# Mixer kernel on one core: two weight groups take one token set first, and the other set is turned by VectorE from stored rows

## The chip, the cores and the metric

The kernel runs on one core of a Trainium2 chip. The time is the device time of one execution in microseconds (us); a run's time is given as the median of several executions. TensorE is called PE, VectorE DVE, ScalarE ACT, GpSimd POOL and SyncE SP, as in the profile.

## The reference

For 2048 tokens u of width 576 (all float32):

```python
xn = layernorm(u)
s  = causal_conv(xn, kernel made from log_A, A_imag, C, log_dt) + xn * D_skip
y  = layernorm(xn)
h  = gelu(y @ w1 + b1)          # 576 -> 4608
g  = silu(h @ w2 + b2)          # 4608 -> 576
out = u + s * g
```

The convolution is a state-space kernel of length 2048 per channel, computed here with Fourier transforms on PE.

## The kernel before, in words

**The two-layer network.** Each float32 product is made of three fast matmuls: an operand is split into a high part (a copy rounded on ACT) and a low part (the rest, on DVE), and high x high, high x low and low x high are summed. The 2048 tokens are done in two halves of 1024, and a half in two token sets of 512. The hidden width 4608 is cut into 12 groups of 3 x 128 units. One group on one set is a slot; there are 48. The order of slots is group by group, set 0 then set 1 (line 1436). A slot has a first layer (`layer1`, L508, 42 matmuls of 512 columns into three hidden blocks) and a second layer (`layer2`, L565, 72 matmuls of 288 columns, each third one with the low part of a hidden block), whose four results DVE adds to `acc` (L573). Between them ACT makes the activation (L541) and the high part `hh` (L544), DVE the low part `hl` (L547), block by block. The weights of a group come by SP in eight parts to a ring (`load_raw`, L448 to L453) and are split by ACT (L488) and DVE (L485) while PE works on the other layer; a new part is loaded when an old one in its place has been split (line 486). 24 groups of weights are loaded, 12 for each half.

**The tokens of a set** must stand with their features on the partitions, as `XH`, `XL` and `XR` (the last 64 features). `norms` makes normalised rows (`second`, L386). In the first half PE turns the rows (`y_transpose`, L413: 4 transposes for each of 5 feature blocks), ACT takes the high part from PSUM (L417, L419) and DVE the low part (L423, L425); `turn_lines(4, 1)` places this for set 1 within slot 0. In the second half the rows are stored to DRAM (`y_s`, L388), loaded in pieces by token blocks (L1231, 32 x 16 x 32 elements) and turned by DVE in blocks of 32 x 32 (L1236).

**The convolution** has a chain of its own: parameters (`params`: four arrays loaded by SP in L681, turned by DVE in L688), tables, kernel spectrum, and on PE short matmuls with small tiles of the array (L869, L941, L979, L1032, L1059), which stand as 87 stretches between the matmuls of the network, the first in slot 9, the last in slot 44. Fifteen of the 87 hold two steps, the others one.

**The order of the work** is made when the program is built. `Order` keeps lines of steps, each with an engine, an allotted time, needs and a due time, and a clock for each engine. PE's matmuls of the network are placed one after another; steps of the other engines go where they begin earliest without making a step with a due time late; `pe_turns` puts convolution and turning steps between the matmuls, at a pace that spreads them up to END = 1020. Loads are steps without an engine: SP's queue gets them in the order in which the planner comes to them, and works them off in that order. Each engine runs its instructions in order.

## Time and profile before

| what | us |
|---|---|
| median of 3 runs (1082.5 to 1084.62) | 1082.88 |
| profiled execution | 1082.74 |
| its span in the profile | 1081.0 |
| PE busy | 1071.7 (99%) |
| DVE busy | 947.9 (88%) |
| ACT busy | 650.7 (60%) |

Busy times are sums over instructions that may overlap on an engine. The span runs from the first to the last instruction; 1.7 us of the execution lie outside it.

### The profile page before, as it was taken

How to read it: one execution, taken by the hardware profiler on the slowest of the kernel's cores; microseconds unless marked ns; L12 is line 12 of the kernel's file. 1: busy time of each engine (PE TensorE's matmuls, PEld its weight loads, DVE VectorE, ACT ScalarE, POOL GpSimd, SP SyncE). 2: the span in 40 equal slices, each digit the busy share in tenths (PEclk: the TensorE clock that was granted, in tenths of full speed). 3: DMA queues.
4: the chain of work that ended last, by engine and by line, in shares of the span. 5: the costliest groups of instructions: out<-in, count | busy, mean ns of one | idle time of the engine just before them, and what ended most of it. 6: DMA issues, size and time to landing. Idle time of an engine off the chain costs nothing.

```text
span 1081.0 us, 27198 instructions
## 1 busy us (share of the span) xinstructions
PE 1071.7 (99%) x11491; PEld 933.9 (86%) x11491; DVE 947.9 (88%) x1518; ACT 650.7 (60%) x974; POOL 199.1 (18%) x281
## 2 busy tenths in 40 slices
PE   9999999999999999999999999999999999999997
PEld 7989999889888888888888888888888887888896
DVE  7797878989999999999999999999999996677366
ACT  6558569767666665767756666576665754233333
POOL 6559342110000200002100010000100022110231
PEclk9999999999999999999999999999999999999999
DMA  7746455823225221455523433142312347332344
GB/s 236 229 140 190 163 186 196 229 71 113 72 71 110 65 80 55 112 94 129 144 59 100 82 86 88 33 124 55 97 53 76 115 85 237 111 111 88 89 156 117
DMA packets 136537, 125.54 MB, mean 116 GB/s; under 512 B 88156, under 2 KB 108096, under 8 KB 135392
## 3 DMA queue, kind: packets, MB, share of 16 engines
q1 hardware_dynamic: 120624, 76.44, 26.2%
q0 software_dynamic: 15040, 46.40, 13.8%
q8 instruction: 90, 1.47, 0.6%
q10 hardware_dynamic: 752, 0.97, 0.3%
q14 instruction: 31, 0.25, 0.1%
HBM read 95.52 MB, written 34.01 MB: 120 GB/s over the span
## 4 chain that ended last, share of the span: by engine, by line
PE 98%; DVE 1%; issue 1%; DMA 0%; ACT 0%; POOL 0%; ACTq 0%; POOLq 0%; DVEq 0%
PE mxa L508 22%; PE mxa L565 21%; PE mxb L565 21%; PE mxb L508 21%; PE cv L869 3%; PE cv L979 3%; PE cv L1032 2%; PE cv L941 2%; PE cv L1059 1%; DMA idp<-in_ident_dram 0%; PE mxa L523 0%; PE cv L413 0%; DVE A L646 0%; DVE row L386 0%; DVE acc L573 0%
## 5 line engine op out<-in xcount | busy, mean ns | idle before, releaser
L565 PE MATMUL mxa<-w2h,hh 128*128 128x288 f32 x573 | 171.3, 299 | 0.0
L565 PE MATMUL mxb<-w2h,hh 128*128 128x288 f32 x576 | 170.9, 297 | 0.0
L565 PE MATMUL mxb<-w2h,hl 128*128 128x288 f32 x576 | 170.0, 295 | 0.0
L565 PE MATMUL mxb<-w2l,hh 128*128 128x288 f32 x576 | 169.6, 294 | 0.0
L565 PE MATMUL mxa<-w2h,hl 128*128 128x288 f32 x573 | 169.1, 295 | 0.0
L565 PE MATMUL mxa<-w2l,hh 128*128 128x288 f32 x573 | 168.7, 294 | 0.0
L547 DVE TENSOR_TENSOR hl<-h,hh 128x512 fp32r<-128x512 f32 x144 | 99.4, 692 | 76.8 <-ACT hh L544 76.1
L541 ACT ACTIVATE h<-mxa,b1t 128x512 f32<-128x512 f32 x73 | 50.2, 690 | 126.3 <-PE mxa L508 121.7
L769 POOL DMA_DIRECT2D par<-par_s x36 | 27.3, 759 | 519.4 <-DVE mg L812 479.7
L565 PEld LDWEIGHTS mxa<-w2h,hh 128*128 128x128 f32 x573 | 107.6, 188 | 9.4 <-issue 6.3
L565 PEld LDWEIGHTS mxb<-w2h,hh 128*128 128x128 f32 x576 | 108.2, 188 | 4.9 <-issue 2.5
L565 PEld LDWEIGHTS mxb<-w2l,hh 128*128 128x128 f32 x576 | 108.1, 188 | 0.6
L565 PEld LDWEIGHTS mxa<-w2l,hh 128*128 128x128 f32 x573 | 107.6, 188 | 0.7
L565 PEld LDWEIGHTS mxb<-w2h,hl 128*128 128x128 f32 x576 | 108.1, 188 | 0.0
L565 PEld LDWEIGHTS mxa<-w2h,hl 128*128 128x128 f32 x573 | 107.5, 188 | 0.0
L541 ACT ACTIVATE h<-mxb,b1t 128x512 f32<-128x512 f32 x71 | 48.9, 689 | 76.9 <-PE mxb L508 76.1
L544 ACT ACTIVATE hh<-h 128x512 fp32r<-128x512 f32 x144 | 90.8, 632 | 4.0
L573 DVE TENSOR_TENSOR acc<-mxa,acc 128x576 f32<-128x576 f32 x88 | 65.4, 743 | 17.0 <-PE mxa L565 16.7
L508 PE MATMUL mxa<-XH,w1h 128*128 128x512 f32 x284 | 80.2, 404 | 0.0
L508 PE MATMUL mxb<-XH,w1h 128*128 128x512 f32 x280 | 77.1, 397 | 0.0
L508 PE MATMUL mxa<-XL,w1h 128*128 128x512 f32 x284 | 76.2, 390 | 0.0
L508 PE MATMUL mxa<-XH,w1l 128*128 128x512 f32 x284 | 76.0, 389 | 0.0
(231 smaller groups left out, 2420.8 us busy)
## 6 DMA issues: line engine op xcount, KB each, us to landing
raw<-in_B_w_dram SPq DMA_DIRECT2D x72, 288.0 KB, 3.3
raw<-in_B_w_dram SPq DMA_DIRECT2D x96, 192.0 KB, 2.9
par_s<-A POOLq DMA_DIRECT2D x8, 1080.0 KB, 5.9
par<-par_s POOLq DMA_DIRECT2D x36, 240.0 KB, 3.3
f2t<-f2q SPq DMA_DIRECT2D x24, 256.0 KB, 3.7
raw<-in_B_w_dram SPq DMA_DIRECT2D x48, 96.0 KB, 3.6
u_s<-in_A_u_dram POOLq DMA_DIRECT2D x16, 288.0 KB, 4.3
xc<-xn_s SPq DMA_DIRECT2D x48, 96.0 KB, 3.8
```

The source lines that it names most:

```text
L508: nc.tensor.matmul(q, a, b, start=j == 0, stop=j == len(ops) - 1)
L541: nc.scalar.activation(t, q, AF.Gelu_apprx_tanh, bias=b1t[:, g * G + i:g * G + i + 1], scale=1.0)
L544: LAST[0] = nc.scalar.activation(hh[:, i], t, AF.Copy)
L547: nc.vector.tensor_sub(hl[:, i], t, hh[:, i].bitcast(F32))
L565: nc.tensor.matmul(q[:, dh, :288], a[:, i, c], b[:, i, d], start=i == 0 and k == 0, stop=i == G - 1 and k == 2)
L573: nc.vector.tensor_add(o, q[:, dh:dh + n, :288], b if g == 0 else o)
L769: nc.gpsimd.dma_start(PAR[b].rearrange("p (g i) k -> p g (i k)", g=4), dram(par_s, (b // 6 * CH + b % 6 * 4) * NPAR, [[D * NPAR, P], [24 * ...
L869: nc.tensor.matmul(q[32 * g:32 * g + 32, i // 2, i % 2 * 64:i % 2 * 64 + 64], U[:, ri, 4 * g + i, :], v[:, ri, 4 * g + i, :], start=ri == ...
L941: nc.tensor.matmul(Q1ST[i, x][g // 2][64 * f:64 * f + 64, g % 2].rearrange(order), f1t[r].rearrange("p s k -> p (s k)"), rhs(r, f), start= ...
L979: nc.tensor.matmul(Q[i][32 * q:32 * q + 32, f, 2 * ri:2 * ri + 2], m[r, 4 * i + q, 32 * ri:32 * ri + 32], A2[r, 4 * p + 2 * i + q // 2, :, ...
L1032: nc.tensor.matmul(QI[q // 2][64 * f:64 * f + 64, q % 2, i], MAT["g2t", p + i // 2][r, i % 2, ri], YS[p + i // 2][0][r, i % 2, ri, f], sta ...
L1059: nc.tensor.matmul(Q[f][32 * e:32 * e + 32, t], g1t[r], A2[r, k:k + 2, 1].rearrange("p i d r -> p i r d"), start=True, stop=True, skip_gro ...
```

## The change

The order of slots becomes a table: groups 0 and 1 on set 0, groups 2 to 11 on both sets, then groups 1 and 0 on set 1; the second half begins with group 0, whose weights stay, and goes on with groups 1 to 11. So set 1 is first used in slot 3 instead of slot 1, and there are 25 loads of a group's weights instead of 24.

Set 1 of the first half is no longer turned by PE. `second` writes its rows with the first 512 features in another order (two instructions for a row: 4 x 4 x 32 elements and 64), SP stores them to a new `y4_s`, and `row_lines` loads them again: for each block of 128 tokens four loads of 32 x 4 x 128 elements (pieces of 512 bytes, L1225 in the new file), and for the last 64 features two loads of 32 x 16 x 32 (L1228). DVE turns them (L1234, L1237), ACT takes the high part (L1248), DVE the low part (L1252). The loads of the rows for the second half (`rest_of_norms`) wait until the fourth of these loads has been issued. Some turns of parameters wait for DVE's turns, whose memory they use. END becomes 990, the pace of the convolution's first step 0.30 of a gap, and `pe_turns` looks at all lines at other places of a slot. The order now has 85 stretches of convolution work, of which 17 hold two steps.

```diff
@@ second @@
-            engine.tensor_scalar(y, XT[b0 + t], mv[:, t, 0:1], rs[:, 1, t:t + 1], op0=OP.subtract, op1=OP.mult)
-            if b0 >= 8:
+            x = XT[b0 + t]
+            parts = [(y, x)]
+            if b0 == 4:
+                m = KB * P
+                parts = [(y[:, :m].rearrange("p (q k j) -> p k q j", q=4, k=KB), x[:, :m].rearrange("p (k q j) -> p k q j", q=4, k=KB)),
+                         (y[:, m:], x[:, m:])]
+            for o, i in parts:
+                engine.tensor_scalar(o, i, mv[:, t, 0:1], rs[:, 1, t:t + 1], op0=OP.subtract, op1=OP.mult)
+            if b0 == 4:
+                nc.sync.dma_start(dram(y4_s, t * P * D, [[D, 64], [64 * D, 2], [1, D]]), y)
+            elif b0 >= 8:
...
-    for half in range(2):
-        for g in range(NG):
-            PARTS += [(half, g, 1, i) for i in range(KB + 1)] + [(half, g, 2, i) for i in range(G)]
+    SETS = [(0, (0,)), (1, (0,))] + [(g, (0, 1)) for g in range(2, NG)]
+    SETS += [(1, (1,)), (0, (1, 0, 1))] + [(g, (0, 1)) for g in range(1, NG)]
+    SEQ = [(n, g, tb) for n, (g, tbs) in enumerate(SETS) for tb in tbs]
+    FIRST, GATE = (0, 3, 2 * NG, 2 * NG + 1), (2 * NG - 4, 2 * NG - 1)
+    for n, (g, _) in enumerate(SETS):
+        PARTS += [(n, g, 1, i) for i in range(KB + 1)] + [(n, g, 2, i) for i in range(G)]
...
-    def turn_lines(b0, tb):
+    def row_lines():
+        Y = [A2F[:, k:k + TB] for k in (2 * D, PT0 + 4 * D, 0, D, PT0 + 4 * D + TB, PT0 + 4 * D + 2 * TB)]
+        X, T = [Y[k] for k in (0, 1, 2, 0, 3)], Y[4:]
+        def load(i):
+            for q in range(4 if i < KB else 2):
+                y = X[i][32 * q:32 * q + 32]
+                if i < KB:
+                    nc.sync.dma_start(y.rearrange("p (b d) -> p b d", b=4), dram(
+                        y4_s, i * P * D + P * q, [[D, 32], [32 * D, 4], [1, P]]))
+                else:
+                    nc.sync.dma_start(y.rearrange("p (b j) -> p b j", j=32), dram(
+                        y4_s, KB * P + 32 * q, [[D, 32], [32 * D, NT], [1, 32]]))
...
+        for i in range(KB + 1):
+            od.line()["steps"].append(step(None, 7.2, lambda: None, need=[("yn", 4 + min(i, 3))], mark=("ys", i)))
+            issue["steps"].append(step(None, 2.1 if i < KB else 1.1, lambda i=i: load(i), mark=("yi", i),
+                                       need=[("ys", i)] + ([("yt", 0)] if i == 3 else [])))
+            od.line()["steps"].append(step(None, 4.6, lambda: None, need=[("yi", i)], mark=("yl", i)))
+            a, b, c = od.line(), od.line(), od.line()
+            a["steps"].append(step("DVE", dve(TB), lambda i=i: blocks(i), mark=("yt", i),
+                                   need=[("yl", i)] + ([("y2", i - 2)] if i > 1 else [])))
+            b["steps"].append(step("ACT", act(TB), lambda i=i: high(i), mark=("yh", i), need=[("yt", i)]))
+            c["steps"].append(step("DVE", dve(TB), lambda i=i: low(i), need=[("yh", i)], mark=("y2", i) if i < KB else ("x", 1)))
+        od.lines = od.lines[-26:] + od.lines[:-26]
...
-    nl["steps"].append(step(None, 7.0, rest_of_norms))
+    nl["steps"].append(step(None, 7.0, rest_of_norms, need=[("yi", 3)]))
...
-    END = 1020.0
+    END = 990.0
...
-        g, tb = slot // 2 % NG, slot % 2
-        n = slot // 2
+        n, g, tb = SEQ[slot]
+        change = slot + 1 < NSLOT and SEQ[slot + 1][0] != n
...
-            pe_turns(all_lines=pos in (0, 1, G + 1, G + 4, NPOS - 1))
+            pe_turns(all_lines=pos in (0, 1, 2, G + 1, G + 3, G + 5, G + 6, NPOS - 1))
```

What the planner makes of it, at three places.

PE at the end of slot 0, before (`cv` is the PSUM tile of the turned rows, `mxa` and `mxb` those of the network):

```order
L565 MATMUL mxa<-w2h,hl 128x288
L413 MATMUL cv<-idp,row 128x128 x16
L565 MATMUL mxb<-w2h,hh 128x288
...
L565 MATMUL mxb<-w2h,hl 128x288
L413 MATMUL cv<-idp,row 64x128 x4
L508 MATMUL mxa<-XH,w1h 128x512 x4
```

In the change no L413 row (L423 in the new file) stands there; only the turning of set 0 ahead of slot 0 is left on PE.

DVE around slot 2's second layer, before (`hl` is the low part of a hidden block, `w2l` of a weight part; `w` holds rows for the second half, `kt` a parameter):

```order
L485 TENSOR_TENSOR w2l<-raw,w2h 128x576 x3
L381 RECIPROCAL U<-U 128x8
L386 TENSOR_SCALAR row<-w,U 128x576
L699 TENSOR_TENSOR kt<-kt,pr 128x576
L386 TENSOR_SCALAR row<-w,U 128x576 x3
L547 TENSOR_TENSOR hl<-h_687,hh 128x512
L371 BN_STATS st<-w 128x6 x2
L373 BN_AGGR U<-st 128x2
L547 TENSOR_TENSOR hl<-h_725,hh 128x512
```

and in the change (`A_81` holds the loaded and turned rows of set 1):

```order
L498 TENSOR_TENSOR w2l<-raw,w2h 128x576
L1234 STREAM_TRANSPOSE A_81<-A_81 128x512
L1237 STREAM_TRANSPOSE A_81<-A_81 64x512
L560 TENSOR_TENSOR hl<-h_694,hh 128x512
L1252 TENSOR_TENSOR XL<-A_81,XH 128x4x128
L1252 TENSOR_TENSOR XR<-A_81,XR 64x512
L702 STREAM_TRANSPOSE A_81<-kt 128x576
L560 TENSOR_TENSOR hl<-h_728,hh 128x512
L372 BN_STATS st<-w 128x6 x2
L374 BN_AGGR U<-st 128x2
```

The last two turns of set 1 now stand ahead of the first `hl` of slot 2, and two low parts and a turn of a parameter ahead of the second; behind the second there are two pairs of statistics, and then the third `hl`.

SP's queue in slots 1 and 2, before (`raw` is a weight part, `pr`, `mg` and `kt` are parameters, `w` and `v` rows for the second half):

```order
L346 DMA w<-in_A_u_dram 128x576 x6
L346 DMA v<-in_A_u_dram 128x576 x2
L681 DMA pr<-in_A_C_real_dram 32x18x32 x4
L448 DMA raw<-in_B_w_dram 128x576 x2
L681 DMA mg<-in_A_C_imag_dram 32x18x32 x4
L448 DMA raw<-in_B_w_dram 128x576
L681 DMA kt<-in_A_A_imag_dram 32x18x32 x4
```

and in the change:

```order
L463 DMA raw<-in_B_w_dram 128x384
L466 DMA raw<-in_B_w_dram 64x384 x2
L1225 DMA A_81<-y_s 32x4x128 x4
L695 DMA pr<-in_A_C_real_dram 32x18x32 x4
L1225 DMA A_81<-y_s 32x4x128 x4
L461 DMA raw<-in_B_w_dram 128x576 x2
L1225 DMA A_81<-y_s 32x4x128 x4
L461 DMA raw<-in_B_w_dram 128x576
L695 DMA mg<-in_A_C_imag_dram 32x18x32 x4
L1225 DMA A_81<-y_s 32x4x128 x4
L1228 DMA A_81<-y_s 32x16x32 x2
L347 DMA w<-in_A_u_dram 128x576 x6
```

The 18 loads of set 1's stored rows (the names `y_s` and `y4_s` print alike) share the queue with eight loads of parameters and the weights of group 2; the rows for the second half moved behind them.

## Rows read from the trace of the kernel before

**Rows 1.** Page, part 1: busy us (share of the span) and instructions of each engine

```profile
PE 1071.7 (99%) x11491; PEld 933.9 (86%) x11491; DVE 947.9 (88%) x1518; ACT 650.7 (60%) x974; POOL 199.1 (18%) x281
```

**Rows 2.** Waits of PE, first and last of three: us in total, times, longest

```profile
PE mxa L1117 <- POOL XL L1111: 1.3, 1, 1.3
...
PE mxa L523 <- ACT XH L417: 0.2, 1, 0.2
```

**Rows 3.** Windows: us, busy PE, PEld, DVE, ACT, POOL; PEclk, DMA share, GB/s

```profile
900.00:1000.00 100.00, 100.00 (x1023) 86.12 (x1007) 68.89 (x129) 31.90 (x64) 15.72 (x30) 1.00 0.43 135
```

**Rows 4.** Timeline of PE, 27 to 36 us: start, us, engine, line, operation

```profile
29.65 0.29 PE L565 MATMUL mxa<-w2h,hl 128*128 128x288 f32 x1
29.79 2.26 PE L413 MATMUL cv<-idp,row 128*128 128x128 f32 x16
31.80 0.38 PE L565 MATMUL mxb<-w2h,hh 128*128 128x288 f32 x1
32.02 0.30 PE L565 MATMUL mxb<-w2l,hh 128*128 128x288 f32 x1
...
34.14 0.29 PE L565 MATMUL mxb<-w2h,hl 128*128 128x288 f32 x1
...
34.62 1.17 PE L508 MATMUL mxa<-XH,w1h 128*128 128x512 f32 x4
```

**Rows 5.** Chain that ended last, merged: start us, us, what

```profile
38.06 3.17 PE mxb L508 x14
```

**Rows 6.** Timeline of PE, 193 to 196 us, round one stretch of L869

```profile
193.50 0.39 PE L508 MATMUL mxb<-XR,w1s 128*128 128x512 f32 x1
193.82 1.10 PE L869 MATMUL cv<-v,U 128*32 128x64 f32 x64
194.85 1.20 PE L508 MATMUL mxa<-XH,w1h 128*128 128x512 f32 x4
195.88 0.39 PE L508 MATMUL mxa<-XL,w1h 128*128 128x512 f32 x1
```

**Rows 7.** Timeline of PE, 63 to 66.6 us: second layer of slot 2

```profile
63.96 0.29 PE L565 MATMUL mxa<-w2h,hl 128*128 128x288 f32 x1
...
65.94 0.29 PE L565 MATMUL mxa<-w2h,hl 128*128 128x288 f32 x1
```

**Rows 8.** Timeline of DVE, 18 to 46 us

```profile
18.33 1.52 DVE L485 TENSOR_TENSOR w2l<-raw,w2h 128x576 fp32r<-128x576 f32 x2
...
21.55 1.29 DVE L547 TENSOR_TENSOR hl<-h,hh 128x512 fp32r<-128x512 f32 x2 [0.72 <-ACT hh L544]
...
29.27 1.08 DVE L386 TENSOR_SCALAR row<-A,U 128x576 f32<-128x576 f32 x2
...
34.47 0.76 DVE L573 TENSOR_TENSOR acc<-mxb,bias 128x576 f32<-128x576 f32 x1 [0.26 <-PE mxb L565]
...
43.27 0.81 DVE L371 BATCH_NORM_STATS2 st<-w 128x6 f32<-128x288 f32 x2
...
44.36 0.82 DVE L371 BATCH_NORM_STATS2 st<-w 128x6 f32<-128x288 f32 x2
...
45.83 0.69 DVE L547 TENSOR_TENSOR hl<-h,hh 128x512 fp32r<-128x512 f32 x1 [0.41 <-ACT hh L544]
```

**Rows 9.** Line L1236: count, ns min/median/max, first and last start, forms

```profile
L1236 DVE STREAM_TRANSPOSE row<-row x10: 667/694/704, 465.5 to 536.2; 128x512 f32<-128x512 f32 x8, 64x512 f32<-64x512 f32 x2
```

**Rows 10.** Timeline of SP's DMA queue, 25 to 60 us

```profile
36.05 4.60 SPq L681 DMA_DIRECT2D pr<-in_A_C_real_dram  x4
...
51.67 2.40 SPq L681 DMA_DIRECT2D kt<-in_A_A_imag_dram  x4
56.13 1.97 SPq L450 DMA_DIRECT2D raw<-in_B_w_dram  x4
```

**Rows 11.** Line L1231: issue ns min/median/max, and issue to landing

```profile
L1231 SPq DMA_DIRECT2D row<-y_s x36: 302/488/1578, 452.7 to 529.5; - x36
...
DMA to landing us min/median/max: 1.9/3.2/5.2
```

More of the change, by code (lines that the diff above doesn't have):

```diff
@@ L556, in layer2 @@
         c = slice(j * P, (j + 1) * P)
+        first = turn[0] - 1 in FIRST
         if alone and terms[0][1]:
@@ L572, in add @@
             b = bias2.rearrange("p (h d) -> p h d", h=2)[:, dh:dh + n]
-            nc.vector.tensor_add(o, q[:, dh:dh + n, :288], b if g == 0 else o)
+            nc.vector.tensor_add(o, q[:, dh:dh + n, :288], b if first else o)
         return add
@@ L687, in params @@
         e, d = act(D) + 0.1, dve(D)
-        turns = lambda k, to: add("DVE", d, lambda: V.transpose(to, T[k]), need=[("praw", k)], at=48.0)
+        turns = lambda k, to: add("DVE", d, lambda: V.transpose(to, T[k]), need=[("praw", k)] + ([("yt", {0: 2, 3: 3, 1: 4}[k])] if k != 2 else []), at=48.0)
         turns(0, nrm)
@@ L1200, in norm_lines, with blocks, places, high @@
             wx["steps"].append(step(None, 5.0, lambda: None, need=[("xs", b0 + t)], mark=("xn", b0 + t)))
-    def turn_lines(b0, tb):
-        x, xh, x2 = nl, nlh, nl2
-        cell = {}
-        def first(k0):
-            for kb in (k0, k0 + 1):
-                if kb <= KB:
-                    cell[kb] = y_transpose(b0, tb, kb)
-                    for i in range(4):
-                        cell[kb][0](i)
-        M = lambda *a: ("turn", tb, b0) + a
-        for ks in ((0, 1), (2, 3), (4,)):
-            x["steps"].append(step("PE", 0.5 * len(ks), lambda k0=ks[0]: first(k0), cv=1,
-                                   need=[M("l", 1)] if ks[0] == KB else (), mark=M("t", ks[0])))
-            for kb in ks:
-                xh["steps"].append(step("ACT", 0.6, lambda kb=kb: cell[kb][1](), need=[M("t", ks[0])], mark=M("h", kb)))
-            for kb in ks:
-                x2["steps"].append(step("DVE", 0.6, lambda kb=kb: cell[kb][2](), cv=-(kb == ks[-1]),
-                                        need=[M("h", ks[-1])], mark=("x", tb) if kb == KB else M("l", kb)))
+    def row_lines():
[10 more added lines that the diff above has]
+                        y4_s, KB * P + 32 * q, [[D, 32], [32 * D, NT], [1, 32]]))
+        def blocks(i):
+            x, y = T[i % 2], X[i]
+            if i < KB:
+                nc.vector.transpose(x.rearrange("p (k b t) -> p k b t", k=4, b=4),
+                                    y.rearrange("p (b k j) -> p k b j", k=4, b=4))
+            else:
+                nc.vector.transpose(x[:64], y[:64])
+        def places(i):
+            y = T[i % 2]
+            c = slice(i * P, (i + 1) * P)
+            if i < KB:
+                return y.rearrange("p (k t) -> p k t", k=4), XH[:, :, 1, c], XL[:, :, 1, c]
+            return y[:64], XR[:64, 1], XR[64:, 1]
+        def high(i):
+            y, h, _ = places(i)
+            nc.scalar.activation(h, y, AF.Copy)
+        def low(i):
+            y, h, lo = places(i)
+            nc.vector.tensor_sub(lo, y, h.bitcast(F32))
+        issue = od.line()
+        for i in range(KB + 1):
[9 more added lines that the diff above has]
+        od.lines = od.lines[-26:] + od.lines[:-26]
@@ L1300, in mixer_kernel @@
     norm_lines(4)
-    turn_lines(4, 1)
+    row_lines()
     def rest_of_norms():
@@ L1368, in pe_turns @@
                     gap = (END - now) / max(pace["left"], 1)
-                    if n == 0 and pace["started"] and now < pace["last"] + 0.4 * gap and not any_time:
+                    if n == 0 and pace["started"] and now < pace["last"] + 0.30 * gap and not any_time:
                         break
@@ L1389, in mixer_kernel @@
     later(mid - 3, 0, block_lines)
-    later(mid - 2, G - 1, lambda: x_free(0))
+    later(mid - 4, G - 1, lambda: x_free(0))
     later(mid - 1, G - 1, lambda: x_free(1))
@@ L1445, in mixer_kernel @@
                     od.force(lambda: all(m in od.marks for m in need))
-                    if slot in (1, 2 * NG + 1):
+                    if slot in (3, 2 * NG + 1):
                         od.marks["x", tb] -= 2.3
@@ L1458, in mixer_kernel @@
                 od.advance(od.t["PE"])
-                if pos == G - 1 and tb == 1 and slot + 1 < NSLOT:
+                if pos == G - 1 and change:
                     weigh_in(1)
@@ L1484, in mixer_kernel @@
                         x["steps"] += st
-                    elif g == NG - 1:
+                    elif slot in GATE:
                         for d in range(2):
@@ L1490, in mixer_kernel @@
                     od.urgent.append((od.t["PE"], chain))
-                if pos == NPOS - 1 and tb == 1 and slot + 1 < NSLOT:
+                if pos == NPOS - 1 and change:
                     weigh_in(2)
```

3 lines of the change are left out of this document (2 added, 1 removed).

## The prediction

> **What bounds the kernel now.** I read the page first: PE is busy 99% of the span [rows 1], and that it hardly ever stands still is shown by the list of PE's waits: three entries in the whole span, all at the start of the kernel, the first and longest 1.3 us, the last 0.2 [rows 2]. The chain that ended last is therefore PE's own stream almost from end to end; no DVE, ACT or DMA work sets the end. DVE comes second, and it has room late: from 900 to 1000 us it is busy 68.89 of 100 us, ACT 31.90 [rows 3]. So two things can change the time: how long PE's stream is, and whether something new makes PE wait. The clock in that window is 1.00 of full speed, the 2.4 GHz level, and PE stays as busy, so the clock is left out.
>
> **The change part by part**
>
> *PE's transposes of set 1 go (20 instructions, two stretches).* In a dense stretch of layer 2 the 15 matmuls from 63.96 to 65.94 us begin 0.132 us apart [rows 7]. From the last matmul ahead of the 16 transposes to the second behind them, 29.65 to 32.02, it takes 2.37 us in place of two such steps, 0.26: the stretch costs 2.11. The second stretch, four transposes, sits between 34.14 and 34.62: 0.48 less 0.13 is 0.35 [rows 4]. Behind any such stretch the next four wide matmuls take longer too: after L869 the step from 194.85 to 195.88 is 1.03 us, where four steps of a clean block (3.17 us for 14, 0.226 each [rows 5]) are 0.91; that adds 0.1 to the second stretch [rows 6]. Sum: 2.11 + 0.35 + 0.1 = **2.55 us gained**.
>
> By the Trainium skill (VectorE: DVE Perf Modes, Rules for kernel authors) a 128 x 128 transpose belongs on TensorE if PSUM is an acceptable destination, which speaks against this change. The trace agrees that one is cheap there: 16 of them hold the stream 2.1 us, about 0.13 each.
>
> *The convolution's stretches go from 87 to 85.* Entering one costs 0.32 rather than 0.23 us (193.50 to 193.82), leaving one the 0.12 just worked out [rows 6]: 0.2 each, two fewer, **0.4 gained**. The matmuls inside are the same.
>
> *One more set of group weights* (25 loads for 24). Eight parts more on ACT and DVE; DVE's cost is 0.76 at most for one (two in 1.52 [rows 8]), so up to 6 us of DVE, as much again of ACT, and four table loads more. No PE time. The work that hides it is the free DVE time late in the kernel [rows 3]: convolution steps slip into it. Without that cover 6 us would show.
>
> *Weights in time for slots 1 and 2.* A group now lasts one slot instead of two. Group 1's first-layer weights must be split by 32 us; SP loads them behind the splits of group 0 at the same place as before, and the last part's split stands ahead of slot 0's last eviction on DVE, which is due at 34.47 - 2.1 = 32.4 [rows 8]. PE begins slot 1 at 34.62 - 2.46 = 32.2 [rows 4] and comes to that part only with its last matmul, 13 x 0.226 later, at 35.1. I take no wait; a slip by the longest issue shown, 1.6 us [rows 11], would still fit.
>
> *Set 1 turned by DVE: where a new wait can arise.* Set 1 itself is needed only in slot 3, past 70 us (72 matmuls of 0.132 after 60.8). The danger is the in-order queue: the last two turns stand ahead of slot 2's first `hl`, and two low parts and a parameter's turn ahead of its second. PE needs the second block's `hl` at 63.96 - 2.55 = 61.4 and the third's at 65.94 - 2.55 = 63.4 [rows 7].
>
> Say the last turn starts at s. DVE does 512 columns at a pace of 0.60 (two in 1.29, the last of them 0.69 [rows 8]; one alone 0.69 for a turn [rows 9]). Turn, `hl`, two low parts: 2.4; parameter's turn 0.7 (estimate, 576 columns); second `hl` 0.6; two pairs of statistics 1.09 each, 43.27 to 44.36 [rows 8], with the aggregate in it: 2.1; third `hl` 0.69. Together 6.5, so s must be **56.9 or earlier**; later counts one for one against PE. Without waits DVE would be there at about 55.5: slot 1's last `hl` ends at 45.83 + 0.69 - 2.55 = 44.0 [rows 8], and between stand five splits of 0.5 (384 columns, estimate), four evictions of 0.67, seven turns and low parts of 0.6 and three splits of 0.7, 11.5 in all.
>
> When are the last two pieces there? SP's queue decides. Its anchor is the load of group 2's fourth part, behind DVE's split of the last of group 1: slot 0's last eviction starts at 34.47 - 2.1 = 32.4; then 0.76, four rows of 0.5 (two in 1.08) with 0.15 each for the new small piece (estimate), two splits 1.52, one `hl` 0.6, one split 0.76: 38.6 [rows 8]. Then SP issues three weight loads at 0.49 (four in 1.97 [rows 10]): 40.1. Then 29 issues: 18 pieces, 8 parameter loads, 3 weight loads. The nearest row for a piece is the same kind of load in the second half: 0.30 at the least, 0.49 in the middle, and 1.9, 3.2 and 5.2 us to landing [rows 11]. With 0.52 from start to start, 0.6 for parameters (four in 2.40 [rows 10]) and 0.43 for weights it is 9.4 + 4.8 + 1.3 = 15.5; the last piece starts at 55.1 and lands at 58.3: a wait of 1.4. Bounds: at 0.35 for a piece and 0.5 for parameters, last start near 51.3 and landing before 55: **no wait**. At 1.15 for a parameter load (four in 4.60 [rows 10]) and 4.3 us to landing: 40.1 + 9.4 + 9.2 + 1.3 - 0.5 + 4.3 = 63.8, **a wait of 7**. I take 1.0, a little under the middle, because 16 of the 18 pieces have 128 runs of 512 bytes rather than 512 runs of 128, and the eight 288 KB row loads that stood ahead of the slow parameter load now stand behind.
>
> The Trainium skill (DMA: Bandwidth & Descriptors, Anatomy of one DMA) puts a DMA at about 2.0 us plus bytes over 436 GB/s; that is for GpSimd's queue, and as an estimate a 64 KB piece would land in 2.15 us. The landing row's middle is 3.2; by the page there would be a wait of only 0.35 and 1080.1 us.
>
> *Sum.* 1082.74 (profiled execution; its span 1081.0, 1.7 us lie outside) - 2.55 - 0.4 = 1079.8 with no wait; + 1.0 = **1080.8 us**. The profiled execution is 0.14 below the median of the runs, which is nothing.
>
> **The rivals**
>
> *The pieces are clearly late* (wait 2 to 5 us): SP at 0.6 per issue throughout, as for the parameters, and 3.2 us to landing put s at 40.1 + 17.4 - 0.6 + 3.2 = 60.1, a wait of 3.2. For it: the queue already spends 2.40 us on four parameter loads, and DVE has only 1.4 us between 55.5 and 56.9. Against: the pieces carry less. Time 1081.8 to 1084.8, 1083.0 by this count: no difference that can be measured.
>
> *Slower: SP's queue blocks DVE's in-order queue for long.* Place: slot 2's second layer. Price: wait less 2.95. It decides from s = 59.9 (level with the profile), and is past the bound from s = 62. With both parameter loads at the slow pace it is 7 us, 1082.74 - 2.95 + 7 = 1086.8. For: such a load is in the trace [rows 10]. Against: only one of the two shown is slow, and it stood behind bulk loads. What the rule on transposes quoted above would come to here is this rival: work taken from the engine that sets the end lands on one whose lateness it then waits for.
>
> *A single-use group once more, at slots 22 and 23*, where groups 1 and 0 follow each other and SP also loads the second half's pieces, whose issue took 1.58 us at worst [rows 11]. Nothing in the trace shows weights late there; a few such issues make 1 to 3 us, 1081 to 1083.
>
> *The wait is not there and the gain is a little larger* (fewer disturbances of PE's pace): 1079.3.
>
> **How the numbers follow.** A measurement of this kernel can tell about 0.2%, 2.2 us, from no change: below 1080.7 is faster, above 1085.0 slower. The forecast, a wait of 0 to 2 us, gets 0.66 (1079.8 to 1081.8); somewhat over half of it, 0.42, has a wait under 0.9 and is faster, 0.24 is within the bound. Late pieces 0.16 (same); blocked queue 0.09 (slower); slots 22 and 23 0.05 (same); larger gain 0.04 (faster). Faster 0.46, same 0.45, slower 0.09. The range 1079.3 to 1083.4 leaves out the blocked queue and the upper part of the late pieces.
>
> **What would show it.** On PE: no L423 after the start, slot 1's first L521 at about 32.2 instead of 34.6, 85 stretches, and slots 4 to 20 without a wait. In SP's queue: the last L1228 issued at about 55 and landed at about 58. On DVE: an idle time before L1234 or L1237 ended by a DMA, and on PE a wait of about 1 us before an L578 with `hl` between 61 and 64 us. Wrong it would be if PE waited for weights in slot 1, 2 or 23, if waits over 2 us showed anywhere else, or if DVE's extra 6 us made PE wait in the second half.

## The result, and the profile after

The changed kernel takes 1087.78 us (median of 6 runs, 1087.32 to 1088.87), the kernel before 1082.98 in the runs made beside it: the ratio is 1.0045, 95% interval 1.0032 to 1.0058. That is slower by 4.8 us; 1080.8 was forecast, with 1079.3 to 1083.4 as the range. The profiled execution has a span of 1085.5 us where 1081.0 stood.

The first part of the page, and the waits of PE (line, releaser: us in total, times, longest), which answer to [rows 1, 2]:

```profile
PE 1072.5 (99%) x11471; PEld 933.4 (86%) x11471; DVE 956.7 (88%) x1535; ACT 660.2 (61%) x988; POOL 197.9 (18%) x281
```

```profile
PE mxb L521 <- ACT h L554: 1.9, 1, 1.9
...
PE mxb L579 <- DVE hl L560: 1.1, 2, 0.6
PE mxa L579 <- DVE hl L560: 0.8, 1, 0.8
PE mxa L579 <- DVE acc L587: 0.5, 1, 0.5
PE mxb L579 <- ACT hh L557: 0.2, 1, 0.2
```

PE has 20 instructions fewer, the transposes, as it should. Five lines of waits are new, six waits with 4.5 us in all, and each is for an engine that feeds the two-layer network (the MLP below) or takes its results: `h` (the gelu, L554) and `hh` from ACT, `hl` and `acc` from DVE. None names weights.

The list of waits shows less than was lost. So I add up over PE's timeline by how much the distance between the starts of neighbouring MLP matmuls exceeds that of an undisturbed pair (0.2265 us for 512 columns, 0.1327 for 288). This also takes in the restart and a lowered clock. In the kernel before, no place behind the start loses as much as 0.25 us. In the changed one it is 4.65 us between 48 and 68, 1.06 at 125 and 162, 2.52 between 474 and 500, together **8.2**. The stretches of other work between MLP matmuls, each with the first step behind it, shrink from 143.9 to 140.8 us by the same count: **3.1 gained**. The balance of 5.1 agrees with what is seen: the last MLP matmul starts at 1078.34 instead of 1073.60, 4.7 later, and the first one 0.2 earlier.

**Slot 2** loses most. PE's timeline there:

```profile
57.94 0.39 PE L521 MATMUL mxa<-XR,w1s 128*128 128x512 f32 x1
60.22 1.46 PE L521 MATMUL mxb<-XH,w1h 128*128 128x512 f32 x4 [1.90 <-ACT h L554]
61.48 1.91 PE L521 MATMUL mxb<-XL,w1h 128*128 128x512 f32 x4
63.19 1.66 PE L521 MATMUL mxb<-XH,w1l 128*128 128x512 f32 x4
...
65.14 0.29 PE L579 MATMUL mxa<-w2h,hh 128*128 128x288 f32 x1
```

PE begins slot 2's third block only when the gelu of the first has read `mxb`, the PSUM tile that both blocks use: 2.28 us from 57.94 to 60.22 instead of 0.23. (The third block writes the other half of that tile, L515; whether the wait could be done without was not tried.) Then the 14 matmuls take 4.92 us (60.22 to 65.14) instead of the 3.17 of [rows 5]. The windows say why (us, PE, PEld, DVE, ACT, POOL, then PEclk, the granted clock):

```profile
58.00:60.00 2.00, 0.32 (x2) 0.00 (x0) 1.75 (x3) 1.97 (x3) 0.00 (x0) 1.00 0.63 128
60.00:62.00 2.00, 1.78 (x6) 1.43 (x7) 1.11 (x3) 1.38 (x4) 0.00 (x0) 0.75 0.99 221
62.00:64.00 2.00, 2.00 (x6) 1.58 (x5) 1.97 (x4) 1.78 (x3) 0.00 (x0) 0.50 0.99 336
64.00:66.00 2.00, 2.00 (x12) 1.75 (x11) 1.97 (x5) 0.66 (x1) 0.00 (x0) 0.90 1.03 385
```

PE stood in the window from 58 to 60, and behind it the clock is 0.50 of full speed, 1.2 GHz. The wait cost 2.05 us and the low clock 1.75 more.

Why the gelu was late stands in the timeline of ACT; the gelu is the last row, its table load the row ahead:

```profile
53.96 0.67 ACT L501 ACTIVATE w2h<-raw 128x576 fp32r<-128x576 f32 x1
54.80 0.69 ACT L501 ACTIVATE w2h<-raw 128x576 fp32r<-128x576 f32 x1 [0.17 <-DMA raw<-in_B_w_dram]
56.96 0.69 ACT L501 ACTIVATE w2h<-raw 128x576 fp32r<-128x576 f32 x1 [1.48 <-DMA raw<-in_B_w_dram]
57.55 0.61 ACT L1248 ACTIVATE XH<-A 128x512 fp32r<-128x512 f32 x1
58.19 1.28 ACT L554 ACT_TABLE_LOAD   x1
59.48 0.69 ACT L554 ACTIVATE h<-mxb,b1t 128x512 f32<-128x512 f32 x1
```

The block was there at about 55.0 (the next one's first matmul starts at 54.99). Ahead of the gelu in ACT's in-order queue stand the third of slot 2's second-layer weight pieces, which lands only at 56.96, a copy of set 1's third piece, and a table load that the parameters' exponential at 49.31 has made necessary.

The kernel before was closer to this wait than its empty list of waits shows. Its PE (second and third block of slot 2), and its ACT:

```profile
56.96 1.07 PE L508 MATMUL mxa<-XH,w1h 128*128 128x512 f32 x4
60.13 1.07 PE L508 MATMUL mxb<-XH,w1h 128*128 128x512 f32 x4
```

```profile
58.73 0.69 ACT L541 ACTIVATE h<-mxb,b1t 128x512 f32<-128x512 f32 x1
```

There too the gelu stands behind the third weight piece (split at 55.58) and a table load (57.43), and starts 1.8 us after its block was there; it ends 0.7 ahead of the third block. In the change the block is there 2.0 us earlier and the gelu starts 0.75 later. So the larger part of the missing time is the gain itself: PE came sooner, and what stands ahead of the gelu did not.

SP's queue in the change shows why that weight piece is late:

```profile
49.91 0.88 SPq L461 DMA_DIRECT2D raw<-in_B_w_dram  x2
50.83 2.14 SPq L1225 DMA_DIRECT2D A<-y_s  x4
53.07 0.38 SPq L461 DMA_DIRECT2D raw<-in_B_w_dram  x1
53.49 2.48 SPq L695 DMA_DIRECT2D mg<-in_A_C_imag_dram  x4
56.06 1.86 SPq L1225 DMA_DIRECT2D A<-y_s  x4
57.97 0.96 SPq L1228 DMA_DIRECT2D A<-y_s  x2
```

It is issued at 53.07, behind four transfers of set 1's third piece, and takes 3.9 us.

The first 0.8 of the 4.65 us, at 48.5 to 49.3, comes ahead of this. The eviction that PE waits for (L587 at 48.51) stands on DVE behind the split of group 2's last first-layer part (48.03), which waited 1.4 us for ACT, and ACT 1.4 us for that part's DMA. At 162, `hl` stands behind steps of the parameters on DVE, which had waited 3.05 us for a DMA at 156.95.

**Slots 21 and 22** lose 2.5 us. DVE's timeline, one row, and then ACT's:

```profile
473.17 0.71 DVE L1280 STREAM_TRANSPOSE row<-row 128x512 f32<-128x512 f32 x1 [0.49 <-DMA row<-y_s]
```

```profile
473.92 0.63 ACT L1285 ACTIVATE XH<-row 128x512 fp32r<-128x512 f32 x1 [0.83 <-DVE row L1280]
474.46 0.61 ACT L557 ACTIVATE hh<-h 128x512 fp32r<-128x512 f32 x1
...
475.32 0.69 ACT L554 ACTIVATE h<-mxa,b1t 128x512 f32<-128x512 f32 x1
```

It is the same picture: ACT stands 0.83 us at the copy of a second-half piece whose turn waits for its DMA, and the `hh` that PE needs, ready since the gelu of 472.40, is behind it. That is 1.4 of the 2.5 us. The other 1.1, at 497 to 500, shows no late transfer right ahead of it: `hl` (499.40) stands behind four steps of the convolution on DVE that begin at 496.94. The pieces are late because SP reads them late, behind one load of the convolution (L933) in its queue, which waits 8.3 us for PE's step L993 (list of SP's waits); the kernel before issued the same load (L919) earlier and the first pieces right after. SP in the change and then before:

```profile
463.69 0.32 SPq L933 DMA_DIRECT2D f2t<-f2q  x1
464.06 11.33 SPq L1275 DMA_DIRECT2D row<-y_s  x15
```

```profile
452.32 0.33 SPq L919 DMA_DIRECT2D f2t<-f2q  x1
452.69 15.46 SPq L1231 DMA_DIRECT2D row<-y_s  x12
```

The planner could not see that the first pieces go out 11 us later: its step for the first two reads has no start date, so to it they have landed from the beginning on, and it put the copies where they suited ACT.

### The profile page after: what moved, and what is told of

The parts are those of the page before. It is cut to its first block, busy times and chain, and to the rows that moved or that the text cites. A ratio compares the mean times of both kernels' runs of the same rounds, so it can differ in the third digit from the quotient of the medians.

```text
span 1085.5 us, 27235 instructions
## 1 busy us (share of the span) xinstructions
PE 1072.5 (99%) x11471; PEld 933.4 (86%) x11471; DVE 956.7 (88%) x1535; ACT 660.2 (61%) x988; POOL 197.9 (18%) x281
## 4 chain that ended last, share of the span: by engine, by line
PE 81%; issue 2%; DVE 2%; DMA 2%; POOL 1%; SPq 1%; ACT 0%; ACTq 0%; DVEq 0%; POOLq 0%
PE mxa L579 18%; PE mxb L579 18%; PE mxb L521 17%; PE mxa L521 17%; PE cv L883 3%; PE cv L993 3%; PE cv L1046 2%; PE cv L955 2%; DMA par_s<-A 1%; PE cv L1073 1%; DMA par<-par_s 1%; DMA row<-y_s 1%; SPq L1275 1%; POOL w L405 0%; POOL v L405 0%
## 5 line engine op out<-in xcount | busy, mean ns | idle before, releaser
L554 ACT ACTIVATE h<-mxa,b1t 128x512 f32<-128x512 f32 x73 | 50.0, 687 | 130.4 <-PE mxa L521 129.4
L554 ACT ACTIVATE h<-mxb,b1t 128x512 f32<-128x512 f32 x71 | 48.8, 687 | 78.0 <-PE mxb L521 76.9
L587 DVE TENSOR_TENSOR acc<-mxa,acc 128x576 f32<-128x576 f32 x88 | 65.4, 743 | 24.0 <-PE mxa L579 23.6
L521 PE MATMUL mxb<-XH,w1h 128*128 128x512 f32 x280 | 78.0, 400 | 1.9 <-ACT h L554 1.9
L521 PE MATMUL mxa<-XH,w1h 128*128 128x512 f32 x284 | 77.8, 396 | 0.0
L587 DVE TENSOR_TENSOR acc<-mxb,acc 128x576 f32<-128x576 f32 x88 | 65.7, 746 | 13.3 <-PE mxb L579 13.0
L521 PE MATMUL mxa<-XL,w1h 128*128 128x512 f32 x284 | 76.0, 389 | 0.0
```

The costliest lines, as they stand in the source:

```text
L521: nc.tensor.matmul(q, a, b, start=j == 0, stop=j == len(ops) - 1)
L554: nc.scalar.activation(t, q, AF.Gelu_apprx_tanh, bias=b1t[:, g * G + i:g * G + i + 1], scale=1.0)
L587: nc.vector.tensor_add(o, q[:, dh:dh + n, :288], b if first else o)
```

## The experiments

**Theory A**: what costs is the order in which the planner put work into ACT's and DVE's in-order queues. It holds transfers for landed that aren't, and the MLP's next gelu or `hl` stands behind them. **Rival B**: a second single-use weight set can't be had in time, whatever the order. **Rival P**: the planner's new pace. **Theory D**: DVE's six further microseconds. Line numbers in e2, e4, e11 and e12 differ by a few from those of the change; the functions are the same. "Lost" is the sum described above, in us, by where in the profile it lies (us; places under 0.25 left out).

| run | us, median | ratio to before (95%) | lost 48-100 | lost 100-170 | lost 470-505 | later |
|---|---|---|---|---|---|---|
| the change | 1087.78 | 1.0045 (1.0032, 1.0058) | 4.65 | 1.06 | 2.52 | 0 |
| e1 | 1093.24 | 1.0096 (1.0079, 1.0113) | 9.93 | 0.90 | 1.92 | 0 |
| e2 | 1091.12 | 1.0073 (1.0055, 1.0091) | 5.18 | 1.76 | 0 | 0.32 (at 388) |
| e3 | 1091.37 | 1.0079 (1.0064, 1.0094) | 4.75 | 1.09 | 4.55 | 0 |
| e4 | 1096.84 | 1.0128 (1.0113, 1.0143) | 4.91 | 1.27 | 9.52 | 0 |
| e5 | 1088.20 | 1.0051 (1.0035, 1.0067) | 4.39 | 3.11 | 1.55 | 0 |
| e6 | 1085.59 | 1.0028 (1.0017, 1.0039) | 3.91 | 0.31 | 2.12 | 0 |
| e7 | 1085.29 | 1.0029 (1.0017, 1.0041) | 4.44 | 0 | 2.79 | 0 |
| e8 | 1087.71 | 1.0049 (1.0033, 1.0065) | 6.37 | 1.01 | 0 | 0 |
| e9 | 1081.76 | 0.9989 (0.9980, 0.9999) | 1.01 | 0 | 0 | 0.46 |
| e10 | 1082.20 | 0.9997 (0.9987, 1.0006) | 0 | 0.51 | 0.80 | 0 |
| e11 | 1082.88 | 1.0001 (0.9992, 1.0010) | 0.77 | 0 | 0 | 0 |
| e12 | 1083.40 | 1.0008 (0.9999, 1.0017) | 0 | 0.36 | 0 | 0 |
| e13 | 1092.38 | 1.0085 (1.0070, 1.0100) | 0 | 0.52 | 0 | 4.27 |
| e14 | 1082.58 | 1.0000 (0.9991, 1.0010) | 0 | 0.52 | 0 | 0 |

**e1, the pieces on another queue.**

```diff
-                    nc.sync.dma_start(y.rearrange("p (b d) -> p b d", b=4), dram(
+                    nc.gpsimd.dma_start(y.rearrange("p (b d) -> p b d", b=4), dram(
...
-                    nc.sync.dma_start(y.rearrange("p (b j) -> p b j", j=32), dram(
+                    nc.gpsimd.dma_start(y.rearrange("p (b j) -> p b j", j=32), dram(
```

> Only the queue is changed that issues the 18 reads of set 1's pieces (GpSimd's in place of SyncE's); the order of work on TensorE, VectorE and ScalarE stays as in the changed kernel. Theory A (the reads stand in SyncE's queue ahead of slot 2's second-layer weights; the third of those lands at 56.9 us, ScalarE's in-order queue stands at it, the gelu of slot 2 that was due at 55.0 starts at 59.5, TensorE stands 1.9 us and then runs at half clock): the third piece is issued some 3 us earlier, TensorE's 1.9 us wait in slot 2 falls under 0.5 and the granted clock stays at 1.0 from 60 to 66; 1083.5 to 1084.5 us. Rival B (the second single-use weight set is too much for ScalarE and VectorE whatever the queue): the wait stays over 1.5 us, 1087 to 1088. Rival C (the pieces themselves, not the weights, are late): the wait moves with them, 1085 to 1087.

1093.24, outside every range; of the three, C named what happened, at far too low a price. The weights did come earlier (third split on ACT at 54.69 instead of 56.96), but GpSimd's queue is in order too. Two of its normalisations and their stores stood ahead of the last pieces, which were issued from 56.67 on, and the turn on DVE waited (DVE's timeline):

```profile
65.01 0.71 DVE L1234 STREAM_TRANSPOSE A<-A 128x512 f32<-128x512 f32 x1 [6.17 <-DMA A<-y_s]
```

ACT's copy behind it started at 65.75, the second gelu at 67.35, and PE stood 5.6 us. The place where PE stands has moved to another consumer of a late transfer; the queue alone is no cure.

**e2, set 1 turned by PE** in the new slot order, rows kept in SBUF.

```diff
-    row_lines()
+    turn_lines(4, 1)
...
-            if b0 == 4:
-                nc.sync.dma_start(dram(y4_s, t * P * D, [[D, 64], [64 * D, 2], [1, D]]), y)
```

> Slot order and weight sets as in the changed kernel, but set 1 is turned by TensorE as in the kernel before (20 transposes and the copies out, rows kept in SBUF, no store and no pieces). Theory A (the pieces cause slot 2's loss of 3.8 us, the middle of the program costs 2.4 us whatever turns set 1): slot 2's wait goes, the transposes cost 2.5 us again, the loss at 470 to 500 us stays: 1085.5 to 1087. Rival B (two single-use weight sets in a row cause it): slot 2 still waits 1.5 us or more, 1088.5 to 1090.5. Rival D (nothing is lost in the middle without the pieces): 1082.5 to 1083.5.

1091.12, above all ranges (the profiled run, span 1087.2, is at the low end of 1088.99 to 1093.17). No pieces, and slot 2 still waits 3.3 us for a gelu. Here the eight 288 KB row loads stood ahead of the weights in SP's queue and four of the parameters' among them (the first of the three splits starts at 56.05), so this run alone can't tell A from B; e12 does. The loss at 470 to 500 is gone here, which A had expected to stay; 1.5 us of wait for another gelu come at 142.

**e3, the planner's pace of before.**

```diff
-    END = 990.0
+    END = 1020.0
...
-                    if n == 0 and pace["started"] and now < pace["last"] + 0.30 * gap and not any_time:
+                    if n == 0 and pace["started"] and now < pace["last"] + 0.4 * gap and not any_time:
...
-            pe_turns(all_lines=pos in (0, 1, 2, G + 1, G + 3, G + 5, G + 6, NPOS - 1))
+            pe_turns(all_lines=pos in (0, 1, G + 1, G + 4, NPOS - 1))
```

> The planner's pace (END 1020, 0.4 of the gap) and the places at which convolution work may be put between matmuls are those of the kernel before; all else as in the changed kernel. Rival P (the new pace crowds VectorE near 120 to 165 and 470 to 500 us): the waits of 0.3 to 1.1 us there go, 1084.5 to 1085.5. Theory A (slot order, pieces and weights cause all of it): within 1.0 us of the changed kernel, 1086.8 to 1088.8.

1091.37, above A's range too: rival P falls, the new pace is the better one here, and what the old one adds is lost at 475 to 482 (4.55 instead of 2.5).

**e4, group 1's visit to set 1 in slot 12.**

```diff
-    SETS += [(1, (1,)), (0, (1, 0, 1))] + [(g, (0, 1)) for g in range(1, NG)]
+    SETS[7:7] = [(1, (1,))]
+    SETS += [(0, (1, 0, 1))] + [(g, (0, 1)) for g in range(1, NG)]
...
-    later(mid - 4, G - 1, lambda: x_free(0))
+    later(mid - 3, G - 1, lambda: x_free(0))
```

(`GATE` follows the slots.)

> Group 1's visit to token set 1 is moved from slot 22 to slot 12, away from the turning of the second half's sets (slots 20 to 23); token set 0 is then free one slot later, as in the kernel before. Theory A (the single-use weight set beside the second half's turning overloads VectorE and ScalarE at 470 to 500 us): the waits of 0.5, 0.9 and 1.1 us there go, at most 0.5 comes at slots 11 to 13, 1085.0 to 1086.0. Rival (the weight set itself costs this wherever it stands): the waits move to slots 11 to 13, 1087 to 1088.

1096.84. The reason that I gave for 470 to 500 us was wrong: without the single-use set there the loss grew to 9.5 us, and slots 11 to 13 lost nothing. The edit also frees set 0 one slot later; which of the two made the loss grow is not separated. DVE's timeline and then ACT's show the chain at its longest:

```profile
471.72 0.71 DVE L1281 STREAM_TRANSPOSE row<-row 128x512 f32<-128x512 f32 x1 [5.89 <-DMA row<-y_s]
475.08 0.71 DVE L1281 STREAM_TRANSPOSE row<-row 128x512 f32<-128x512 f32 x1 [2.64 <-DMA row<-y_s]
475.71 1.18 DVE L802 TENSOR_TENSOR w<-par,tv 128x1024 f32<-128x1024 f32 x1
...
477.42 0.68 DVE L805 TENSOR_TENSOR w<-w,par 128x512 f32<-128x512 f32 x1
```

```profile
478.13 1.06 ACT L808 ACTIVATE w<-w 128x1024 int32<-128x1024 f32 x1 [8.99 <-DVE w L805]
479.09 0.67 ACT L555 ACTIVATE h<-mxb,b1t 128x512 f32<-128x512 f32 x1
```

Two turns wait 8.5 us for their pieces, a table step of the convolution stands behind them on DVE, ACT waits 9 us for that step, and the gelu is behind it: 4.9 us of wait on PE. It is theory A's mechanism, in the second half's turning.

**e5, slot 2's first gelu ahead of the third weight piece.**

```diff
-                    od.marks["raw", j] = od.t["DVE"] + dve(n) + 5.5 + 1.0 * (j - k0)
+                    od.marks["raw", j] = od.t["DVE"] + dve(n) + (8.5 if 44.0 < od.t["DVE"] < 56.0 else 5.5) + 1.0 * (j - k0)
```

> The planner is told that the second-layer weight pieces asked for between 44 and 56 us land 3 us later than it assumed; it then puts slot 2's first gelu ahead of the third of them in ScalarE's queue, and no transfer is issued at another time up to there. Theory A (ScalarE's in-order queue stands at a late piece with the gelu behind it): the gelu starts at 56.5 to 57.5 instead of 59.5, TensorE's wait of 1.9 us falls under 0.4, the granted clock stays at 1.0, and the 3.8 us of slot 2 shrink to under 1: 1083.5 to 1085. Rival (the weights are late in themselves): TensorE waits the same time a few us later, at the second layer, for the third piece's low part: 1087 to 1088.5.

1088.20 lies in the rival's range, but the picture is neither's: the gelu starts at 59.49, as late as ever, and PE waits 2.6 us. Another late transfer took the place of the one removed (ACT's timeline):

```profile
56.97 0.63 ACT L1248 ACTIVATE XH<-A 128x512 fp32r<-128x512 f32 x1 [2.29 <-DVE A L1234]
57.51 0.67 ACT L501 ACTIVATE w2h<-raw 128x576 fp32r<-128x576 f32 x1
58.19 1.28 ACT L554 ACT_TABLE_LOAD   x1
59.49 0.69 ACT L554 ACTIVATE h<-mxb,b1t 128x512 f32<-128x512 f32 x1
```

The copy of set 1's third piece is still ahead, and its turn waited for the DMA on DVE.

**e6, the parameters' reads 16 us later.**

```diff
-        fetch = [step(None, 6.0, lambda k=k: load(k), at=t, mark=("praw", k)) for k, t in ((0, 28.0), (2, 42.0), (3, 48.0), (1, 54.0))]
+        fetch = [step(None, 6.0, lambda k=k: load(k), at=t, mark=("praw", k)) for k, t in ((0, 28.0), (2, 58.0), (3, 64.0), (1, 70.0))]
```

> The three later reads of the parameters (4 transfers each on SyncE's queue) are planned 16 us later, so that they stand no longer between set 1's pieces and slot 2's weights. Theory A: the third weight piece is issued 1 to 2 us earlier and lands near 55.5, the gelu starts at 58 to 58.5, TensorE's wait falls to 0.5 to 1.0 us and the clock dips less or not: 1084.5 to 1086.5, if later work on the parameters does not stall TensorE in its place (rival: it does, near 125 to 165 us; 1087 or more).

1085.59, in A's range. The third weight piece lands at 55.28, the gelu starts at 57.80, PE waits 1.0 us and the clock stays at 1.00. But the parameters are now themselves a late transfer, with the eviction that PE waits 1.7 us for behind them (DVE's timeline):

```profile
69.53 0.78 DVE L702 STREAM_TRANSPOSE xc<-pr 128x576 f32<-128x576 f32 x1 [2.71 <-DMA pr<-in_A_C_real_dram]
...
70.86 0.75 DVE L587 TENSOR_TENSOR acc<-mxb,acc 128x576 f32<-128x576 f32 x1
```

**e7, the first exponential after slot 2's gelus.**

```diff
-        add("ACT", act(D), lambda: nc.scalar.activation(dt, dt, AF.Exp), tbl="exp", late=0.0)
+        add("ACT", act(D), lambda: nc.scalar.activation(dt, dt, AF.Exp), tbl="exp", late=0.0, at=64.0)
```

> The first exponential of the parameters (with a table load of 1.28 us ahead of it, and another before the next gelu) is planned after slot 2's gelus. Theory A: third weight piece as late as before (56.9), but no table load behind it: the gelu starts at about 58.2, TensorE's wait is 0.6 us instead of 1.9, the clock dips less or not: 1084.5 to 1086.5. Rival (the table loads lie in time in which ScalarE waits for the piece anyway): under 0.5 us of change, 1087 to 1088.3.

1085.29, in A's range. The weight piece is as late (57.29), the gelu follows at 58.40 without a table load, PE waits 1.3 us, not 0.6, and the clock stays at 1.00. Then an `hl` is late by 1.3, DVE being behind the last pieces. A table switch costs ACT 1.29 us here, from the start of the load to that of the next activation (58.19 to 59.48 in the change). The Trainium skill (ScalarE: Activation LUTs, What ACT_TABLE_LOAD costs) puts a switch at about 2.66 us, 1.28 for the load and 1.38 for a drain; no drain shows here.

**e8, the second half's pieces told later.**

```diff
-        ks = [(tb, kb) for tb in range(2) for kb in range(KB + 1)]
+        ks, now = [(tb, kb) for tb in range(2) for kb in range(KB + 1)], od.t["PE"]
...
-            yl["steps"].append(step(None, 5.5, lambda k=k: load(*k), need=[("yt",) + ks[n - 2]] if n > 1 else (), mark=("yl",) + k))
+            yl["steps"].append(step(None, 7.0, lambda k=k: load(*k), at=now, need=[("yt",) + ks[n - 2]] if n > 1 else (), mark=("yl",) + k))
```

> The planner is told that the reads of the second half's pieces begin when they are issued (slot 21) and take 7 us, where it took them for landed already; it then puts slot 21's gelus ahead of the first two copies of set 0's pieces in ScalarE's queue. Theory A (the same mechanism as in slot 2: an in-order queue stands at a late piece ahead of the gelu): the waits of 0.4, 0.8 and 1.0 us at 474 to 500 us go; 1085 to 1086, unless set 0 is then late for slot 24 (a wait of several us ahead of 540 us; rival, 1088 or more).

The loss at 474 to 500 us is gone, 2.5 to 0, as A says. The pieces are no earlier for it (SP's queue):

```profile
465.71 5.98 SPq L1275 DMA_DIRECT2D row<-y_s  x8
```

They go out 1.65 us later than in the change, and PE does not wait there. So it is not their lateness alone that costs, but where their copies and turns stand (the planner moved other steps with them). The time is 1087.71 all the same, outside the range: slot 2, where the program is the same as the change's, lost 6.4 us in this profile instead of 4.65 (PE waited 3.0). The four runs spread over 3.3 us (1085.97 to 1089.31): that loss differs from run to run.

**e9, e5 to e8 together**, the parameters read 14 us later and expected after 11 us. The diffs of e5, e7 and e8, and:

```diff
-        fetch = [step(None, 6.0, lambda k=k: load(k), at=t, mark=("praw", k)) for k, t in ((0, 28.0), (2, 42.0), (3, 48.0), (1, 54.0))]
+        fetch = [step(None, 11.0 if k else 6.0, lambda k=k: load(k), at=t, mark=("praw", k)) for k, t in ((0, 28.0), (2, 56.0), (3, 62.0), (1, 68.0))]
```

> The edits of e5, e6, e7 and e8 together (the planner told later landings for slot 2's second-layer weights, for the parameters and for the second half's pieces; parameters read 14 us later and expected 5 us later still; first exponential after slot 2's gelus). Theory A (all of the loss is in-order queues that stand at transfers the planner held for landed; the extra weight set itself costs nothing): slot 2 loses under 0.8 us, 470 to 500 us under 0.5, the clock stays at 1.0: 1079.8 to 1082.0, at or under the kernel before. Rival B (the second single-use weight set cannot be had in time: first-layer pieces split, second-layer pieces read into the same buffer, split, within one slot): TensorE still waits 1.5 us or more in slot 2 whatever stands ahead of the gelus: 1083.5 to 1086.

1081.76 us: 6.0 us under the change with the same slot order, weight sets and turning, and 1.2 under the kernel before, by an interval that just leaves out 1. The gelu of slot 2 starts 1.8 us after its block was there, as in the kernel before (ACT's timeline):

```profile
56.01 0.67 ACT L554 ACTIVATE h<-mxb,b1t 128x512 f32<-128x512 f32 x1
```

The clock stays at 1.00, and of PE's waits for ACT and DVE behind the start two are left (list of PE's waits):

```profile
PE mxa L579 <- DVE hl L560: 0.5, 1, 0.5
PE mxa L521 <- ACT h L554: 0.2, 1, 0.2
```

Slot 2 lost 1.0 us and not under 0.8, the rest of A's numbers hold; B falls.

**e10, set 1's pieces told 1.9 us later too.** On e9:

```diff
-            od.line()["steps"].append(step(None, 4.6, lambda: None, need=[("yi", i)], mark=("yl", i)))
+            od.line()["steps"].append(step(None, 6.5, lambda: None, need=[("yi", i)], mark=("yl", i)))
```

> As e9_all_three, and the planner also takes set 1's pieces to land 1.9 us later, which puts the third piece's copy behind slot 2's first gelu. Theory A: as e9 or up to 1 us better, 1079.5 to 1081.5. Rival B: 1083.5 to 1086, as e9. Rival C (set 1 is then late for slot 3): a wait of over 0.5 us ahead of slot 3 at about 70 us, 1082 to 1083.5.

1082.20, above A's range and without C's wait at slot 3. Slot 2 loses nothing; 0.8 us come at 493 and two stalls of 0.8 and 0.6 in convolution stretches. The profiled execution took 1084.39, near the top of the ten runs.

**e11, control: the four diffs of e9 in the kernel before.**

> Control: the kernel before with the planner edits of e9 alone (parameters read and expected later, first exponential after slot 2's gelus, later landings for slot 2's weights and the second half's pieces), slot order and TensorE's turning of set 1 untouched. Theory A (before loses nothing to late transfers, so these edits have nothing to give back): 1082.0 to 1083.5, no change. Rival (the edits themselves make e9 faster, not the changed order with them): 1080.5 to 1081.8, and then e9 is no better than this.

1082.88, ratio 1.0001: the edits have nothing to give there. What e9 gains on the kernel before does not come from them alone. It is little, and e10 and e14, other plans of the same change, do not show it (0.9997 and 1.0000).

**e12, the four diffs of e9 in e2's kernel.**

> e9_all_three with set 1 turned by TensorE (20 transposes) as in e2, no store and no pieces. Theory A (the sum of the prediction: transposes 2.5 us of TensorE, all else hidden once the planner knows the landings): 2 to 3 us above e9, 1083.8 to 1084.8, with slot 2's wait under 0.5 us. Rival B (the weights of two single-use sets come too late even without the pieces): slot 2 waits 1.5 us or more, 1085.5 to 1087.5.

1083.40, 1.6 us above e9 (2.1 by the two ratios), a little under A's range. PE's waits are those of the start alone: with two single-use weight sets and 25 loads nothing waits, so **the extra weight set costs PE no wait**, and B falls here too. Its two stretches of transposes cost 2.2 us. By the count above the stretches of other work take 143.4 us against e9's 141.6, 88 in both, and e9 gives back 1.1 of these 1.8 in what it still loses (1.5 against 0.4).

**e13 and e14**, e10 with another landing time for the second half's pieces (e14: 5.5).

```diff
-            yl["steps"].append(step(None, 7.0, lambda k=k: load(*k), at=now, need=[("yt",) + ks[n - 2]] if n > 1 else (), mark=("yl",) + k))
+            yl["steps"].append(step(None, 9.0, lambda k=k: load(*k), at=now, need=[("yt",) + ks[n - 2]] if n > 1 else (), mark=("yl",) + k))
```

> As e10, but the second half's pieces are expected 9 us after their read is planned instead of 7. Theory A (e10's remaining loss, 0.8 us at 493 and stalls of 0.8 and 0.6 us in convolution stretches, comes from where the planner puts work around the second half's turning): slot 2 without a wait as in e10, those gone or moved: 1080.0 to 1081.8. Rival (a spread of about 1 us between any two plans, whatever the landings): 1081.5 to 1083.

> As e10, but the second half's pieces are expected 5.5 us after their read is planned (the figure of the changed kernel, here from the moment of issue). Theory A (the copies go again ahead of slot 21's gelus, since the landing was 6 to 9 us after the first issue): waits of 0.5 to 2 us near 470 to 480 us: 1081.5 to 1083.5. Rival: no wait there, 1080 to 1081.5, and the start of the reads alone was the planner's error.

e13 missed by 10 us: set 1 is now turned too late for slot 25 (list of PE's waits).

```profile
PE mxa L521 <- DVE XR L1294: 2.4, 1, 2.4
```

With the low clock behind it that is 4.3 us, and the span ends some 7 us further behind the last matmul than in the others. There the chain that ended last is no longer the MLP's: DVE stands 3.3 us at the load of the last rows for the output sum (`g_s`, L626), and two steps on DVE and the stores follow. e14 gave 1082.58, a time in A's range, with its rival's picture, no wait in the middle: SP issued the first pieces at 453.56. Its last MLP matmul starts at 1071.96 us, 1.6 ahead of the kernel before, but the span ends 0.2 ahead only; the tail behind it is 1.4 longer. Two steps of the same sum (L626, L627 at 1071.06 and 1071.64, 0.55 us each) stand on DVE ahead of the last evictions there; in the kernel before the last of them is at 1063. So where the planner puts work still moves the time by about a microsecond, with no MLP wait to show for it.

## Why the prediction was wrong

- *PE's transposes and the convolution's stretches, 2.55 and 0.4 gained*: right. No L423 after the start, 85 stretches, slot 1's first L521 at 31.96 (32.2 was forecast); 3.1 us by the distances of matmuls, of which the transposes are 2.5 in the kernel before.
- *One more set of weights, no PE time*: right. DVE does 8.8 us more (956.7 against 947.9) and ACT 9.5, and e12 has no wait. e9 keeps DVE as busy as the change (957.1) and has 0.7 us of waits left, so theory D falls too.
- *Weights in time for slots 1 and 2*: right for slot 1. **For slot 2 this is where it failed first**: only the first-layer weights of group 1 were worked out. Slot 2's second-layer pieces were there at 53.96 to 56.96, before PE's second layer was due (about 61), but the last not before ACT came to it, with slot 2's gelu behind. The last first-layer part of slot 2 cost 0.8 through an eviction.
- *Set 1 turned by DVE, a wait of 1.0 at the second layer*: **the step that failed**. It followed DVE's queue, and asked when `hl` would be there. A late weight piece, the same pieces' copies and a table load stand in ACT's queue, ahead of a gelu that is due at 55.0, six microseconds before the `hl` that I looked at. The forecast moved PE's need of `hl` forward by the 2.55 us gained, but not its need of the gelu, which in the kernel before had 0.7 us to spare. So the place was wrong (first layer, L521; the waits of 1.0 for `hl` in slot 2 did not come), the size (2.05 us), and the clock was left out altogether (1.75 more). Slot 7 waits 0.5 us at 162, where slots 4 to 20 were to be without a wait. The dates of the pieces were off by 3 us too: the last was issued at 58.4 instead of 55.1 and turned at 61.21 instead of 58.3. Two of the three lie in the anchor (SP was done with the weights at 42.2, not 40.1). The price of one piece held: 325, 431 and 616 ns for issue and 2.2, 3.3 and 5.3 us to landing, shortest, middle and longest (SP's line L1225, all 16 of it).

```profile
L1225 SPq DMA_DIRECT2D A<-y_s x16: 325/431/616, 42.2 to 57.5; - x16
...
DMA to landing us min/median/max: 2.2/3.3/5.3
```

- *The DMA estimate of 2.15 us* from the Trainium skill (DMA: Bandwidth & Descriptors, Anatomy of one DMA) comes to the shortest landing measured here (2.2); the middle, 3.3, is 1.1 above it.
- *The rival "SP's queue blocks DVE's in-order queue", 1086.8 us at 9 in 100*, came nearest: the right cause and sign, the wrong engine. *"A single-use group once more at slots 22 and 23", 1 to 3 us*, had the size right (2.5) by luck: it thought of late weights and slow issues. e4 took the group away and the loss grew; e8 moved the copies of the pieces and it went. The two came together, and no case of the forecast had both.
- *The rule on transposes* (the Trainium skill, VectorE: DVE Perf Modes, Rules for kernel authors) speaks against the change. The runs do not bear it out here, where PE sets the time, but by little: with both kernels planned alike, DVE's turning (e9, 1081.76) comes out 1.6 us under PE's (e12, 1083.40). Other plans with DVE's turning (e10, 1082.20; e14, 1082.58) are nearer to it, so how much of it the turning makes is not shown.

So the forecast's sum left out what stands ahead of PE's next need. With a planner that expects later landings, e9, the kernel takes 1081.76, still 1.0 above the forecast.

## What to carry to other kernels

Where one engine sets the time and the others run in-order queues that a planner fills, ask of each transfer not only whether its data are there when they are *used*, but what stands behind the instruction that consumes them, on every engine that touches them; in the change the harm was done in ACT's queue more than in DVE's. A list without waits says nothing of how near one is: when the engine that sets the time gets faster, look up how much each of its needs had to spare. Cutting one late transfer out hands the wait to the next in line (e5 to e8 gave back at most 2.5 us each, together 6.0), so correct the planner's landing times together, from the SP rows of a profile, before judging the change. A wait of PE must be priced with what the clock does after it.
